# Copying attention's output out of PSUM in one piece, phi's exponentials on VectorE, and zero matmuls in TensorE's idle time

## The chip, the cores and the metric

The kernel runs on one core of one Trainium2 chip. The metric is device time in microseconds (us) of a whole execution; lower is better. The span of a profile is 1.5 to 2 us shorter than the time of the same execution.

## The reference

Two attention blocks read their own inputs of 2048 rows x 1024 columns with 32 heads of 32, and their outputs are laid side by side.

```python
# A: plain attention
qkv = (x @ wqkv).reshape(B, S, 3, H, Dh)
p = softmax(q @ k.T * Dh ** -0.5)
a = (p @ v) @ wo
# B: four segments of 512, causal attention inside a segment, plus a linear memory of the earlier ones
phi = lambda t: where(t > 0, t + 1.0, exp(t))
a_dot = softmax(q_s @ k_s.T * scale + mask) @ v_s
a_mem = (phi(q_s) @ M) / (phi(q_s) @ z + 1e-06)
o = g * a_mem + (1 - g) * a_dot          # g = sigmoid(beta), one per head
M, z = M + phi(k_s).T @ v_s, z + phi(k_s).sum()
b = o @ wo
out = concatenate([a, b])
```

## The kernel before

A small planner runs while the program is built. Generators ask for operations and for buffers (`yield do(...)`, `yield acq(...)`); the planner keeps a clock with an assumed cost for each operation and records one fixed order for each engine. Between the instructions stand waits on semaphores. In the trace of the kernel before, the 23164 records of TensorE and the 1302 of VectorE come in the program's order, compared by their lines of code (one TensorE record is missing): nothing was reordered, and where a wait was not over the engine stood, TensorE for 1.44 us before the scores at 701.76 us.

Four heads are worked on at once. The kernel uses PSUM as eight banks: six, in three pairs, hold scores; the other two (`side`) serve everything else: the accumulation of output and denominator (PV), the projections, the memory of B and the output projection.

```python
PAIRS = [(0, 1), (2, 3), (4, 5)]      # banks of scores
OB, SB = 6, 7                         # Pool "side": all other matmuls
par = dict(b=(14, 10, 3), mem=-4, ..., rate=0.6, ahead=20, sl=5, pv=18, ..., off=0.75, oks=(1, 4, 6), ..., od=8, run=4)
```

A batch of scores fills two pairs; each pair is then emptied by one exponential of 128 x 1024 on ScalarE. For 43 pairs the second half goes to VectorE instead, which computes the exponential with six instructions of bit arithmetic and a polynomial:

```python
def exps(self, u, k, x, pr, sl, one):
    ...
    if (u, k, x) in self.off:                      # 43 of 1184
        Q.spawn(self.exps_dve(pr[1], ...))
        yield do("ACT", ... activation(half, self.ps[:, pr[0], :], ACTF.Exp, scale=sc), ...)
        yield ("ev", other + (0,))                 # the pair is free when VectorE has read it
        Q.give(self.pairs, [pr])
    else:
        yield do("ACT", ... activation(ap, self.ps[:, pr[0]:pr[1] + 1, :], ACTF.Exp, scale=sc), ...)
        Q.give(self.pairs, [pr])
```

When a unit of PV is finished (128 times), one side bank holds the output in its first 256 columns and the denominator in the other 256. Four VectorE operations work on it, and the bank is free only after the last:

```python
def finish(self, u, half, OB, tb):
    den, o = self.ps[:, OB, QU:2 * QU], self.ps[:, OB, 0:QU]
    yield do("DVE", ... transpose(Dt, den) ...)
    yield do("DVE", ... reciprocal(Rc, Dt[:, 0:QU:32]) ...)
    yield do("DVE", ... transpose(Rb, spread(Rc)) ...)
    yield do("DVE", ... tensor_tensor(OTA[...], o, Rb, ALU.mult) ...)
    Q.give(self.side, [OB])                        # only here
```

phi of B takes its exponential on ScalarE (32 instructions), then two VectorE operations:

```python
yield do("ACT", ... activation(self.E[:, k0:k1, :], KQ[:, k0:k1, :], ACTF.Exp) ...)
yield do("DVE", ... tensor_scalar(E, E, 1.0, None, ALU.min) ...)
yield do("DVE", ... scalar_tensor_tensor(PH, KQ, 0.0, E, ALU.max, ALU.add) ...)
```

## Time and profile before

| | before |
|---|---|
| time, median of the first 3 runs | 1156.84 us (1154.09 to 1157.5) |
| span of the profile | 1153.8 us |
| first to last softmax exponential | 16.3 to 1137.9 us |
| mean granted TensorE clock (share of full speed) | 0.985 |

From the page of the kernel before, the busy times by engine and, as the second line, the shares of the chain that ended last:

```profile
PE 1050.9 (91%) x23164; PEld 507.3 (44%) x23165; DVE 626.9 (54%) x1302; ACT 1103.9 (96%) x1223; POOL 127.4 (11%) x285
...
ACT 55%; PE 32%; DVE 7%; DMA 4%; issue 1%; SPq 0%; POOL 0%; DVEq 0%
```

ScalarE (ACT) is busy nearly throughout, but the chain runs through TensorE (PE) for a third of the span: ScalarE's row of exponentials is often released by matmuls.

The groups of ScalarE and VectorE (DVE), shapes kept apart. After the count stand the busy time and the mean length in ns of one, then idle time just before them:

```profile
L891 ACT ACTIVATE PT<-ps 128x1024 bf16<-128x1024 f32 x1125 | 1045.3, 1101 | 21.3 <-PE ps L864 19.2
L885 ACT ACTIVATE PT<-ps 128x512 bf16<-128x512 f32 x43 | 32.0, 744 | 0.0
L718 ACT ACTIVATE E<-KQB 128x1024 bf16<-128x1024 bf16 x16 | 18.1, 1131 | 0.0
L718 ACT ACTIVATE E<-KQB 128x512 bf16<-128x512 bf16 x16 | 11.0, 685 | 0.0
...
L1021 DVE STREAM_TRANSPOSE Rb<-Rall 128x256 f32<-128x256 f32 x128 | 57.0, 445 | 4.2
L1018 DVE STREAM_TRANSPOSE Dt<-ps 128x256 f32<-128x256 f32 x128 | 56.4, 441 | 24.2 <-PE ps L994 23.3
L1025 DVE TENSOR_TENSOR OTA<-ps,Rb 128x256 bf16<-128x256 f32 x64 | 27.1, 423 | 2.1
L1019 DVE RECIPROCAL Rall<-Dt 128x8 f32<-128x8 f32 x128 | 25.8, 202 | 4.0
```

Two readings need care. The mean of one exponential (1101 ns) is not its price: neighbours overlap. In the trace's records the distance from start to start, where nothing was waited for, is 0.904 us for 128 x 1024 and 0.478 us for a half; phi's two forms take 0.947 and 0.520 us. And a group can show no idle time while its engine waits: waits shorter than the overlap (about 0.2 us) vanish in "busy". So throughout this text **work at pace** is the sum of counts times these distances, and **ScalarE's waits** is what the start-to-start distances between the first and the last exponential have beyond that. The whole stretch from the first to the last I call ScalarE's row. Before: 1140 distances x 0.904 + 43 x 0.478 + 16 x 0.947 + 16 x 0.520 = 1075 us of work, 46 us of waits, of which 15 follow the 43 halves.

The four operations that hold the side bank add up to 0.44 + 0.20 + 0.45 + 0.42 = 1.51 us.

Some windows of 20 us: busy time and, in brackets, instructions of PE, PEld, DVE, ACT and POOL, then granted TensorE clock, DMA share, GB/s:

```profile
140.00:160.00 20.00, 18.01 (x404) 8.76 (x396) 11.70 (x25) 18.64 (x22) 1.61 (x4) 0.91 0.36 64
700.00:720.00 20.00, 17.35 (x384) 8.73 (x384) 12.78 (x27) 18.37 (x21) 0.65 (x2) 0.91 0.25 55
740.00:760.00 20.00, 16.08 (x336) 7.32 (x332) 10.27 (x20) 18.69 (x21) 0.00 (x0) 0.91 0.52 94
```

A clock of 0.91 over 20 us is one stretch of 3.4 us at half clock (the trace grants 0.5 for 3.41 us from 148.8 us, from 701.8 us and from 756.4 us). What comes just before such a stretch shows in TensorE's timeline (start, length, engine and line, shape, count, and in brackets the idle time before it and who ended it):

```profile
699.93 0.40 PE L864 MATMUL ps<-QA,KA 32*128 32x256 bf16 x8 [0.38 <-ACT PT L891]
701.76 0.61 PE L864 MATMUL ps<-QA,KA 32*128 32x256 bf16 x8 [1.44 <-ACT PT L891]
702.31 0.41 PE L994 MATMUL ps<-PT,VB 128*32 128x256 bf16 x4
702.49 0.43 PE L994 MATMUL ps<-PT,ones 128*32 128x256 bf16 x4
```

Scores, then 1.44 us of nothing, then scores again: between two batches no other matmul stood in the order; as I read it, because no side bank was free in the plan. Four PV matmuls then take 0.41 us where they take 0.28 us at full clock (as at 42 us in the same trace).

### The profile page before, as it was taken

What the parts mean: (1) busy time and instruction counts of PE and PEld (TensorE: products, weight loads), DVE (VectorE), ACT (ScalarE), POOL (GpSimd) and SP (SyncE); (2) the same over time, 40 slices, a digit from 0 to 9 for tenths busy, and PEclk for the clock granted to TensorE, in tenths of its full rate; (3) what the DMA queues carried; (4) which work ended last, traced back from release to release, by engine and by line L of the source; (5) the groups of instructions that cost most, each with busy time, mean ns of one, the idle gap of its engine ahead of it and who ended that gap; (6) DMA issues with size and microseconds to landing.
All of it is one profiled execution on the core that took longest, in us unless ns stands there. A gap on an engine that the chain in (4) does not pass through costs nothing.

```text
span 1153.8 us, 49786 instructions
## 1 busy us (share of the span) xinstructions
PE 1050.9 (91%) x23164; PEld 507.3 (44%) x23165; DVE 626.9 (54%) x1302; ACT 1103.9 (96%) x1223; POOL 127.4 (11%) x285
## 2 busy tenths in 40 slices
PE   7899998988999988988998998989999899899997
PEld 3444443444444444444444444434444444444454
DVE  1235446545566665755657666556656656635342
ACT  4999999999999999999999999999999999999995
POOL 1001102002011011111111111111111111100000
PEclk9999999999999999999999999999999999989999
DMA  9431342232122122242222232341123111211111
GB/s 178 98 67 36 71 120 49 62 70 62 44 58 48 44 64 46 57 71 48 52 49 57 41 61 48 57 76 44 39 53 63 40 42 30 63 52 39 44 40 51
DMA packets 214841, 67.28 MB, mean 58 GB/s; under 512 B 203872, under 2 KB 212064, under 8 KB 214624
## 3 DMA queue, kind: packets, MB, share of 16 engines
q1 hardware_dynamic: 213296, 63.20, 26.1%
q8 instruction: 184, 3.01, 1.1%
q10 hardware_dynamic: 1328, 0.79, 0.2%
q14 instruction: 33, 0.27, 0.1%
HBM read 36.70 MB, written 8.39 MB: 39 GB/s over the span
## 4 chain that ended last, share of the span: by engine, by line
ACT 55%; PE 32%; DVE 7%; DMA 4%; issue 1%; SPq 0%; POOL 0%; DVEq 0%
ACT PT L891 52%; PE ps L612 12%; PE ps L994 9%; PE ps L864 6%; PE ps L1062 4%; DMA xB<-in_B_x_dram 2%; ACT E L718 1%; DVE Rb L1021 1%; DVE Dt L1018 1%; DMA VA<-VT 1%; DVE ze L916 1%; DVE VT L618 1%; DMA PKt<-PH 1%; ACT PT L885 1%; POOL PT L900 0%
## 5 line engine op out<-in xcount | busy, mean ns | idle before, releaser
L891 ACT ACTIVATE PT<-ps 128x1024 bf16<-128x1024 f32 x1125 | 1045.3, 1101 | 21.3 <-PE ps L864 19.2
L994 PE MATMUL ps<-PT,ones 128*32 128x256 bf16 (+1 forms) x4800 | 296.3, 274 | 0.0
L994 PE MATMUL ps<-PT,VA 128*32 128x256 bf16 x4032 | 252.6, 278 | 17.1 <-ACT PT L891 7.7
L864 PE MATMUL ps<-QA,KA 32*128 32x256 bf16 x4096 | 206.3, 276 | 47.7 <-ACT PT L891 42.6
L612 PE MATMUL ps<-xB,WB 128*32 128x512 bf16 x3072 | 208.1, 387 | 12.0 <-DMA xB<-in_B_x_dram 3.5
L612 PE MATMUL ps<-xA,WA 128*32 128x512 bf16 x3072 | 200.5, 381 | 2.1 <-DVE VT L618 0.5
L900 POOL TENSOR_SCALAR_AFFINE_SELECT PT<-PT 128x256 bf16<-128x256 bf16 (+1 forms) x224 | 99.5, 445 | 835.8 <-ACT PT L891 829.4
L864 PEld LDWEIGHTS ps<-QA,KA 32*128 32x128 bf16 x4096 | 61.0, 92 | 214.6 <-ACT PT L891 192.8
L994 PEld LDWEIGHTS ps<-PT,VA 128*32 128x32 bf16 x4032 | 107.9, 97 | 84.1 <-issue 25.9
L994 PEld LDWEIGHTS ps<-PT,ones 128*32 128x32 bf16 x4800 | 129.9, 98 | 24.5 <-issue 0.3
L612 PEld LDWEIGHTS ps<-xB,WB 128*32 128x32 bf16 x3072 | 72.2, 97 | 92.3 <-issue 45.8
L612 PEld LDWEIGHTS ps<-xA,WA 128*32 128x32 bf16 x3072 | 71.0, 96 | 79.6 <-issue 25.3
L618 DVE CAST VT<-ps 128x512 bf16<-128x512 f32 x64 | 44.1, 688 | 105.9 <-PE ps L612 102.2
L618 DVE CAST KQB<-ps 128x512 bf16<-128x512 f32 x64 | 44.1, 689 | 103.0 <-PE ps L612 103.0
L1068 DVE CAST outsb<-ps 128x512 bf16<-128x512 f32 x61 | 42.1, 690 | 106.6 <-PE ps L1062 106.3
L1018 DVE STREAM_TRANSPOSE Dt<-ps 128x256 f32<-128x256 f32 x128 | 56.4, 441 | 24.2 <-PE ps L994 23.3
L1062 PE MATMUL ps<-WoB,OTB 128*32 128x512 bf16 x1024 | 67.1, 381 | 0.5 <-DVE md L742 0.2
L1062 PE MATMUL ps<-xA,OTA 128*32 128x512 bf16 x1024 | 65.0, 381 | 0.3 <-DVE outsb L1068 0.2
L1021 DVE STREAM_TRANSPOSE Rb<-Rall 128x256 f32<-128x256 f32 x128 | 57.0, 445 | 4.2
L994 PE MATMUL ps<-PT,VB 128*32 128x256 bf16 (+1 forms) x768 | 46.2, 267 | 8.2 <-DVE OTA L1025 3.2
L864 PE MATMUL ps<-KQB 32*128 32x128 bf16 (+3 forms) x512 | 43.4, 302 | 3.9 <-ACT PT L891 2.9
L619 DVE TENSOR_SCALAR QA<-ps 128x512 bf16<-128x512 f32 x32 | 22.0, 688 | 41.0 <-PE ps L612 41.0
(76 smaller groups left out, 658.5 us busy)
## 6 DMA issues: line engine op xcount, KB each, us to landing
WB<-in_B_wk_dram SPq DMA_DIRECT2D x32, 256.0 KB, 3.0
WB<-in_B_wq_dram SPq DMA_DIRECT2D x32, 256.0 KB, 2.9
WB<-in_B_wv_dram SPq DMA_DIRECT2D x32, 256.0 KB, 3.3
out_dram<-outsb SPq DMA_DIRECT2D x64, 128.0 KB, 1.8
WA<-in_A_wqkv_dram SPq DMA_DIRECT2D x23, 256.0 KB, 3.1
WoB<-in_B_wo_dram SPq DMA_DIRECT2D x1, 2048.0 KB, 9.6
xA<-in_A_wo_dram SPq DMA_DIRECT2D x1, 2048.0 KB, 8.4
OTA<-in_A_x_dram ACTq DMA_DIRECT2D x2, 256.0 KB, 4.8
```

The lines of the kernel that those rows point to most:

```text
L612: ins = e.matmul(self.ps[32 * c:32 * c + 32, bank, :], W[:, i, 32 * c:32 * c + 32], x(i), start=(i == 0), stop=(i == NI - 1))
L618: return e.tensor_copy(dst, self.ps[:, bank, :])
L619: return e.tensor_scalar(dst, self.ps[:, bank, :], scale, None, ALU.mult)
L718: yield do("ACT", lambda e: e.activation(self.E[:, k0:k1, :], KQ[:, k0:k1, :], ACTF.Exp), r=kq, w=["E"], cost=0.093 + 0.427 * nk, prio=-1)
L864: ins = e.matmul(self.ps[:, bk, col:col + w], lhs(t, hs), rhs(q0, w, hs), start=True, stop=True)
L891: yield do("ACT", lambda e: e.activation(ap, self.ps[:, pr[0]:pr[1] + 1, :], ACTF.Exp, scale=sc), r=[("ps", bk) for bk in pr], w=keys, cos ...
L900: yield do("POOL", lambda e, m=m, n=n: e.affine_select(m, m, pattern=[[0, n], [1, P]], compare_op=ALU.is_ge, fill=0.0, base=0, channel_mul ...
L994: ins = e.matmul(out, l, r, start=st, stop=sp)
L1018: yield do("DVE", lambda e: e.transpose(Dt[:, :], den), r=[("ps", OB)], w=[("Dt", x)], cost=dve(QU), prio=0, hold=0.15)
L1021: yield do("DVE", lambda e: e.transpose(Rb[:, :].rearrange("p (a b) -> p a b", b=32), self.spread(Rc)), r=[("Rc", ui % 64)], w=[("Rb", x)] ...
L1062: ins = e.matmul(self.ps[32 * c:32 * c + 32, bank, :], lhs(j)[:, 32 * c:32 * c + 32], W(j), start=(j == 0), stop=(j == NG - 1))
L1068: return f(self.outsb[ob][:, :], self.ps[:, bank, :])
```

## The change

The intent: give the side bank back after one copy, so that TensorE always has other work between batches of scores; take phi's exponentials off ScalarE; put the 43 softmax halves back on ScalarE (`off=0`); try to keep TensorE's clock up with matmuls of zero weights in planned idle time; and fit the planner's numbers again.

```diff
-    par = dict(b=(14, 10, 3), mem=-4, ..., rate=0.6, ahead=20, sl=5, pv=18, ..., lead=6, ..., wob=80, off=0.75, oks=(1, 4, 6), sh=4, ..., run=4)
+    par = dict(b=(12, 7, 2), mem=4, ..., rate=0.58, ahead=28, sl=4, pv=24, ..., lead=5, ..., wob=40, off=0, oks=(1, 4), sh=2, ..., run=6, po=(1, 1), fp=2, fil=0.65, fs=0.15)
@@ finish
-        den = self.ps[:, OB, QU:2 * QU]
-        o = self.ps[:, OB, 0:QU]
-        yield do("DVE", lambda e: e.transpose(Dt[:, :], den), r=[("ps", OB)], ...)
+        o = OD[:, 0:QU]
+        yield do("DVE", lambda e: e.tensor_copy(OD[:, :], self.ps[:, OB, :]), r=[("ps", OB)], w=[("OD", x), ("Rb", x)], ...)
+        Q.give(self.side, [OB])
+        yield do("DVE", lambda e: e.transpose(Dt[:, :], Rb), r=[("Rb", x)], ...)
         ... reciprocal, transpose, multiply as before, now from OD in SBUF
-            Q.give(self.side, [OB])
+            Q.give(self.ods, [x])
@@ b_mem (phi)
-        yield do("ACT", lambda e: e.activation(self.E[:, k0:k1, :], KQ[:, k0:k1, :], ACTF.Exp), ...)
+        yield do("DVE", lambda e: e.tensor_scalar(E, KQ[:, k0:k1, :], -84.5, 0.0, ALU.max, ALU.min), ...)
+        for k in range(k0, k1):
+            yield do("DVE", ... tensor_scalar(self.ze, Ek, ONE / math.log(2.0), BIAS, ALU.mult, ALU.add) ...)
+            yield from self.power(Ek, ek, 4)       # the five other steps of exps_dve
@@ planner: when TensorE has nothing ready
+            if eng == "PE" and self.fill:
+                rq = self.fill(soon)               # 4 matmuls of zero weights, if less than 65% of
+                if rq:                             # the last 3.4 us was planned busy; added to an
+                    best = (None, rq)              # open accumulation, so they change nothing
... (cut: more buffers for tB, OD in place of Rb and md, the bookkeeping of open accumulations)
```

## The prediction

> **What bounds the kernel now.** ScalarE's exponentials. The table of busy time has ACT at 1103.9 of 1153.8 us (96%); the chain of waits is 55% ACT. From start to start, an unhindered 128x1024 exponential takes 0.904 us, a 128x512 half 0.478, phi's forms 0.947 and 0.520. The first exponential starts at 16.3 us, the last ends at 1137.9. Between them, work at those paces is 1141 x 0.904 + 43 x 0.478 + 16 x 0.947 + 16 x 0.520 = 1075 us; the other 46 us are ACT waiting: 15 after the 43 halves whose partner goes to VectorE (they come out at 0.836 us, hardly below a full one), 30 after full ones, mostly for the next scores. The tail is 16 us.
>
> **Clock.** Nine stretches inside run at half clock (0.91 to 0.93 in 20-us windows). Each follows 3.4 us in which matmuls filled under 0.38 of TensorE's time (typical: 0.78). [...] In these stretches and the 6 us after them ACT lost 13 us of the 46.
>
> **What the change does** (counted in the two programs' instruction orders).
> - ACT: the 43 softmax halves return to ACT (43 full, no halves), phi's 32 exponentials leave. Work at pace: 1184 x 0.904 = 1070.5 us, only 4 us less. But the 15 us of waits behind halves go.
> - VectorE: minus 43 power chains of 3.57 us (154 us), plus 48 (172 us), plus 128 copies of 128x512 out of PSUM at 0.69 us (88 us): 627 becomes about 735 us, 65%. Not the bound.
> - The output bank is freed after 0.69 us instead of 0.44+0.20+0.45+0.42 = 1.51 us of four operations, 128 times.
> - TensorE: 256 zero matmuls in 64 groups, about 7 us.
> - New order: TensorE work queued between two batches of scores exceeded 1.6 us (estimated from column counts) in 33 places before, now in 3: the start, one early place, and one about three quarters through, where 6.8 us of projections precede a unit of B (K and Q come late, behind the reload of x, which took 8 to 9 us before). There ACT will stand for 5 to 9 us.
>
> **Sum.** Start 16.3 + 1070.5 + tail 17 (the copy adds 0.7 to the last chain) = 1104. Waits: 7 at the late unit, 3 at remaining half-clock stretches, about 10 small ones: 1124, against 1153.8. Nearly all the gain is waiting, not work, and all on the critical path. Most comes from the smoother order that early bank release and the dropped halves allow; fillers give perhaps 5 us, phi's move 4 to 5.
>
> **Prediction: 1125 us**, 8 in 10 between 1110 and 1141. Faster by over 2% 0.76, within 2% 0.22, slower 0.02.
>
> **Right if** ACT has 1184 exponentials at 0.904, no phi, busy about 98%; its waits in sum fall from 46 to 15 to 28 us; mean granted clock rises from 0.985 to at least 0.992, with four stretches or fewer below full; VectorE busy 720 to 750; one visible ACT hole near three quarters.
>
> **Wrong if** VectorE, in order and with chains of 3.6 us, holds back evacuations so that TensorE, also in order, brings scores late; or if the fixed order, fitted to assumed costs, meets late transfers of x and weights and the half clock returns; or the zero matmuls stand before scores that are ready.

## The result, and the profile after

The four runs of the changed kernel had a median of 1140.82 us (1137.05 to 1141.11), those of before 1157.17 us. The ratio is 0.9852, interval 0.9819 to 0.9884: 1.5% less time. Ratios here are the mean time of one kernel's fast runs over that of the other's of the same rounds, so not quite the ratio of the medians quoted. The profiled execution was the fastest of the four: a span of 1135.3 us at a clock of 0.997; the others had 0.993 to 0.994.

The page of the changed kernel, the same two lines:

```profile
PE 1052.0 (93%) x23420; PEld 510.5 (45%) x23421; DVE 719.5 (63%) x1459; ACT 1093.5 (96%) x1192; POOL 140.8 (12%) x286
...
ACT 85%; PE 8%; DVE 3%; SPq 1%; DMA 1%; issue 1%; POOL 0%
```

The chain is now 85% ScalarE: matmuls mostly no longer release the exponentials. The groups, read as before:

```profile
L946 ACT ACTIVATE PT<-ps 128x1024 bf16<-128x1024 f32 x1168 | 1073.1, 1180 | 15.2 <-PE ps L919 15.0
...
L1078 DVE COPY OD<-ps 128x512 f32<-128x512 f32 x128 | 87.1, 681 | 24.4 <-PE ps L1051 23.4
L1084 DVE STREAM_TRANSPOSE OD<-Rall 128x256 f32<-128x256 f32 x128 | 56.6, 442 | 3.4
L1081 DVE STREAM_TRANSPOSE Dt<-OD 128x256 f32<-128x256 f32 x128 | 55.5, 434 | 2.4
L981 DVE SCALAR_TENSOR_TENSOR we<-ue 128x512 f32<-128x512 f32 x48 | 34.3, 715 | 0.0
```

Reading from SBUF makes the transposes no faster (434 against 441 ns); the copy is pure extra work of 87 us on VectorE, and it holds the bank for 0.68 us instead of 1.51. The same windows:

```profile
140.00:160.00 20.00, 19.53 (x460) 9.73 (x456) 12.23 (x28) 20.00 (x23) 1.21 (x3) 1.00 0.31 61
700.00:720.00 20.00, 17.28 (x384) 8.14 (x388) 14.37 (x29) 19.84 (x23) 5.35 (x9) 1.00 0.22 48
740.00:760.00 20.00, 19.23 (x452) 9.55 (x444) 15.40 (x32) 20.00 (x23) 0.00 (x0) 1.00 0.22 48
```

The clock is full and ScalarE has no gap. The larger gaps that are left stand in two places of ScalarE's timeline:

```profile
31.54 24.07 ACT L946 ACTIVATE PT<-ps 128x1024 bf16<-128x1024 f32 x26
57.89 1.94 ACT L946 ACTIVATE PT<-ps 128x1024 bf16<-128x1024 f32 x2 [2.29 <-PE ps L919]
60.93 1.94 ACT L946 ACTIVATE PT<-ps 128x1024 bf16<-128x1024 f32 x2 [1.10 <-PE ps L919]
65.87 20.27 ACT L946 ACTIVATE PT<-ps 128x1024 bf16<-128x1024 f32 x22 [3.00 <-PE ps L919]
...
857.08 10.19 ACT L946 ACTIVATE PT<-ps 128x1024 bf16<-128x1024 f32 x11 [6.40 <-PE ps L919]
```

The second place, 6.4 us before 857, is the late unit of B that the order had shown in advance. The first is explained by TensorE's timeline there:

```profile
53.38 0.29 PE L1051 MATMUL ps<-PT,VA 128*32 128x256 bf16 x3
55.55 0.27 PE L1051 MATMUL ps<-PT,VA 128*32 128x256 bf16 x1 [1.88 <-issue]
...
65.21 0.28 PE L1051 MATMUL ps<-PT,ones 128*32 128x256 bf16 x1 [2.92 <-issue]
```

TensorE stops inside a group of four matmuls that no semaphore divides, "issue" meaning that it waited for nothing the profile shows. This was not foreseen.

ScalarE's account for the profiled execution of every kernel, in us (lead: up to the first exponential; tail: from the start of the last one; parts may miss the span by under 1 us). A profiled execution is not the median one: that of the changed kernel is 3.8 us faster than its kernel's median, that of a_again 1.7 us slower, that of b_off0 1.0 us slower, that of a_old_par_phi_act 2.4 us faster; so differences of 2 or 3 us between two rows say little.

| kernel | lead | work at pace | waits | tail | span |
|---|---|---|---|---|---|
| before | 16.3 | 1074.8 | 46.3 | 17.0 | 1153.8 |
| after | 16.1 | 1069.6 | 33.0 | 16.6 | 1135.3 |
| a_again | 15.8 | 1069.6 | 39.2 | 16.7 | 1140.7 |
| a_ghost_fill | 16.6 | 1069.6 | 33.7 | 16.8 | 1136.7 |
| a_old_finish | 15.9 | 1069.6 | 60.1 | 25.0 | 1170.7 |
| a_phi_act | 15.9 | 1093.1 | 31.4 | 16.7 | 1156.5 |
| a_old_par | 16.1 | 1069.6 | 34.8 | 16.0 | 1135.9 |
| a_old_both | 15.7 | 1069.6 | 54.1 | 15.7 | 1154.7 |
| b_off0 | 15.9 | 1093.1 | 32.8 | 15.9 | 1157.2 |
| a_old_par_phi_act | 16.2 | 1093.1 | 26.3 | 15.7 | 1150.7 |
| a_no_hole | 16.6 | 1069.6 | 27.7 | 15.7 | 1129.1 |
| a_beta | 17.0 | 1069.6 | 30.3 | 17.0 | 1133.2 |
| a_best | 16.4 | 1069.6 | 20.8 | 16.1 | 1122.2 |
| b_fill_fixed | 17.1 | 1074.8 | 43.2 | 16.9 | 1151.9 |

### The profile page after: what moved, and what is told of

Its sections match the earlier page's. It is cut to its first block, busy times and chain, and to the rows that moved or that the text cites. A ratio compares the mean times of both kernels' runs of the same rounds, so it can differ in the third digit from the quotient of the medians.

```text
span 1135.3 us, 50446 instructions
## 1 busy us (share of the span) xinstructions
PE 1052.0 (93%) x23420; PEld 510.5 (45%) x23421; DVE 719.5 (63%) x1459; ACT 1093.5 (96%) x1192; POOL 140.8 (12%) x286
## 4 chain that ended last, share of the span: by engine, by line
ACT 85%; PE 8%; DVE 3%; SPq 1%; DMA 1%; issue 1%; POOL 0%
ACT PT L946 84%; PE ps L655 3%; PE ps L1051 2%; PE ps L1125 2%; PE ps L919 1%; SPq L620 1%; DVE we L981 0%; DMA OTA<-in_A_x_dram 0%; DVE we L982 0%; DMA VA<-VT 0%; DMA PKt<-PH 0%; DVE OD L1078 0%; ACT OTA L946 0%; DVE PH L983 0%; DVE ze L980 0%
## 5 line engine op out<-in xcount | busy, mean ns | idle before, releaser
L946 ACT ACTIVATE PT<-ps 128x1024 bf16<-128x1024 f32 x1168 | 1073.1, 1180 | 15.2 <-PE ps L919 15.0
L919 PE MATMUL ps<-QA,KA 32*128 32x256 bf16 x4096 | 204.0, 273 | 34.0 <-ACT PT L946 26.7
L955 POOL TENSOR_SCALAR_AFFINE_SELECT PT<-PT 128x256 bf16<-128x256 bf16 (+1 forms) x224 | 108.4, 492 | 841.1 <-ACT PT L946 836.2
L655 PE MATMUL ps<-xA,WA 128*32 128x512 bf16 x3072 | 205.6, 382 | 1.8 <-DVE KQB L661 0.9
L655 PE MATMUL ps<-xB,WB 128*32 128x512 bf16 x3072 | 204.0, 382 | 3.2 <-DVE OD L1078 0.9
L1078 DVE COPY OD<-ps 128x512 f32<-128x512 f32 x128 | 87.1, 681 | 24.4 <-PE ps L1051 23.4
L1084 DVE STREAM_TRANSPOSE OD<-Rall 128x256 f32<-128x256 f32 x128 | 56.6, 442 | 3.4
L1081 DVE STREAM_TRANSPOSE Dt<-OD 128x256 f32<-128x256 f32 x128 | 55.5, 434 | 2.4
```

Of the source, the lines that this page charges most:

```text
L655: ins = e.matmul(self.ps[32 * c:32 * c + 32, bank, :], W[:, i, 32 * c:32 * c + 32], x(i), start=(i == 0), stop=(i == NI - 1))
L919: ins = e.matmul(self.ps[:, bk, col:col + w], lhs(t, hs), rhs(q0, w, hs), start=True, stop=True)
L946: yield do("ACT", lambda e: e.activation(ap, self.ps[:, pr[0]:pr[1] + 1, :], ACTF.Exp, scale=sc), r=[("ps", bk) for bk in pr], w=keys, cos ...
L955: yield do("POOL", lambda e, m=m, n=n: e.affine_select(m, m, pattern=[[0, n], [1, P]], compare_op=ALU.is_ge, fill=0.0, base=0, channel_mul ...
L1078: yield do("DVE", lambda e: e.tensor_copy(OD[:, :], self.ps[:, OB, :]), r=[("ps", OB)], w=[("OD", x), ("Rb", x)], cost=dve(2 * QU), prio=0 ...
L1081: yield do("DVE", lambda e: e.transpose(Dt[:, :], Rb), r=[("Rb", x)], w=[("Dt", x)], cost=dve(QU), prio=self.par["fp"], hold=0.15)
```

## The experiments

My theory after the result: the gain is removed waiting, which the early release of the side bank makes possible; phi's move and the fillers add something. The main rival: the fillers keep the clock up (0.985 to 0.994 in the median run), and that is the gain. Names beginning with a_ start from the changed kernel, with b_ from the kernel before. All twelve kernels gave correct results.

### The changed kernel again: a_again

No edit.

> The changed kernel once more, as the yardstick for the three that run beside it. Both theories: 1137 to 1142 us, 0.985 of before, granted clock 0.993 to 0.997, ScalarE's waits between its first and last exponential 33 us or a few more.

Measured: 1140.78 us, ratio 0.9858. It is the yardstick for the next three, which ran beside it.

### The fillers planned but not emitted: a_ghost_fill

TensorE's order without the zero matmuls is the same to the last instruction.

```diff
-        op = self.R.add("SP" if rq.kb else eng, rq.fn, rq.r, rq.w, rq.order, eng)
+        if best[0] is None:
+            op = Op(eng, -1, rq.fn)          # takes its time in the plan, emits nothing
+        else:
+            op = self.R.add("SP" if rq.kb else eng, rq.fn, rq.r, rq.w, rq.order, eng)
```

> The changed kernel with its order kept, but the 64 groups of zero matmuls planned and not emitted. Main theory (gain is the smoother order, which the early bank release allows; fillers are worth about 5 us): 1143 to 1147 us, granted clock 0.988 to 0.992, three to five half-clock stretches more than with fillers. Rival (the clock held up by fillers is the gain): clock back at 0.985 and 1152 to 1157 us. A third outcome, fillers worth nothing: 1139 to 1142, the same clock.

Measured: 1140.57 us, ratio 0.9868, against 1140.78 us beside it; median clock 0.992 against 0.9935. This is the third outcome: in the changed order the fillers are worth nothing that can be measured. My 5 us for them was wrong, and so is the rival: the clock rose because of the order, not because of the fillers.

### The old four operations in PSUM: a_old_finish

The four operations also get back the rank that they had in the planner (`prio=0` instead of `fp`).

```diff
-        yield do("DVE", ... tensor_copy(OD, self.ps[:, OB, :]) ...)
-        Q.give(self.side, [OB])
-        ... transpose, reciprocal, transpose, multiply from OD
+        ... transpose, reciprocal, transpose, multiply from self.ps[:, OB, :], then Q.give(self.side, [OB])
```

> The changed kernel with one part undone: output and denominator are again worked on in PSUM by four VectorE operations, which hold the bank. Main theory: TensorE has fewer banks to work in, so scores come late; 1152 to 1162 us, ScalarE's waits 50 us or more, VectorE busy about 635 us. Rival (fillers, or phi's move, are the gain, the copy is a cost of 88 us of VectorE for nothing): 1136 to 1142 us.

Measured: 1169.83 us, ratio 1.0111: 29 us slower than with the copy, and slower than the kernel before. I had expected 1152 to 1162; the direction is the theory's, the size larger. ScalarE's waits are 60 us, the tail is 8 us longer. Who holds TensorE up shows in its waits in this run (total us, times, longest):

```profile
PE ps L920 <- ACT PT L947: 36.3, 83, 1.4
PE ps L1052 <- DVE tB L1104: 14.6, 22, 1.8
PE ps L1052 <- DVE OTA L1087: 6.1, 8, 1.9
```

and in the changed kernel:

```profile
PE ps L919 <- ACT PT L946: 30.8, 87, 0.8
PE ps L1051 <- ACT PT L946: 9.3, 30, 0.5
PE ps L1051 <- DVE OD L1078: 7.3, 18, 1.1
```

PV waits up to 1.9 us for the multiply that frees the bank; with the copy it waits at most 1.1 us. And while all waits of scores for ScalarE are at most 0.8 us with the copy, they reach 1.4 us without: then, as I read it, TensorE has nothing else it may do, as in the kernel before.

### phi back on ScalarE: a_phi_act

```diff
-    po=(1, 1)
+    po=(0, 1)     # the branch of the changed kernel that keeps the ScalarE exponential
```

> The changed kernel with phi's exponentials back on ScalarE (32 of them, 23.5 us at pace). Main theory: ScalarE is the bound and its waits do not absorb this, so 1157 to 1164 us, as slow as before: phi's move is worth about 20 us, more than the 4 to 5 us of the prediction, which booked it together with the returning halves. Rival (ScalarE's waits absorb half, because the waits come from TensorE's side): 1146 to 1152 us.

Measured: 1156.23 us, ratio 0.9992. The whole gain is gone; the time lies 1 us under the 1157 to 1164 us that the theory gave, and outside the rival's range. The work at pace is 23.5 us more, the waits are 31.4 us instead of 39.2. So with the copy in place phi's move is worth 15.5 us (1156.23 - 1140.78).

### The square of copy and phi

Both parts seem to carry the whole gain, each by itself. To see them apart from the new numbers of the planner I put the old numbers back (`b`, `mem`, `rate`, `ahead`, `sl`, `pv`, `lead`, `wob`, `run`), with no softmax half on VectorE in any corner.

```diff
 a_old_par          = after,  par: numbers of before, off=0
 a_old_both         = a_old_par, and finish() of before
 a_old_par_phi_act  = a_old_par, and po=(0, 1)
 b_off0             = before, par: off=0.75 -> off=0        (both parts old, no fillers)
```

> The changed kernel with the numbers of its planner set back to those of before, except that no softmax half goes to VectorE. The copy out of PSUM, phi on VectorE and the fillers stay. Theory (the early bank release itself lets TensorE be kept in work, whatever the numbers): 1135 to 1146 us. Rival (the new numbers carry the gain): 1150 us or more.

Measured: 1138.65 us, ratio 0.9852. The new numbers carry nothing: with the old ones the ratio is the same as that of the changed kernel (0.9858 in a_again).

> The same old planner numbers, and the old four operations in PSUM as well; phi on VectorE and the fillers stay, no halves. It shows whether the 29 us that the old operations cost under the new numbers are theirs, or come from numbers that were fitted to the copy. Theory (bank release is worth much under either numbers): 1150 to 1160 us, ScalarE's waits 45 us or more. Rival (the 29 us were mostly a misfit of numbers): 1140 to 1147 us.

Measured: 1155.09 us, ratio 0.998, with 54 us of waits. The old operations cost 16 us under the old numbers, 29 under the new ones; the difference goes with the numbers, which had been fitted to the copy. Not all of the 16 us need be the bank's either: this order has a late unit of B of its own, which a_old_par's has not. In ScalarE's timeline:

```profile
861.68 9.27 ACT L947 ACTIVATE PT<-ps 128x1024 bf16<-128x1024 f32 x10 [6.17 <-PE ps L920]
```

> The kernel before with its 43 softmax halves back on ScalarE and nothing else. Work at pace rises by 18.3 us, the 15 us of waits behind halves go. Theory (the halves gained almost nothing): 1150 to 1162 us, ScalarE's waits 25 to 35 us. Rival (the halves were worth their work at pace): 1168 to 1176 us.

Measured: 1157.94 us, ratio 1.0013. The halves had taken 18.3 us of work off ScalarE (43 x (0.904 - 0.478)) and gained nothing clear of noise, as expected: waits fell from 46.3 to 32.8 us when they were undone. The median clock rose to 0.990 against 0.983 beside it, and no time was gained: a higher clock alone is not the gain.

> Completes a square of two by two under the old planner numbers, no softmax half on VectorE in any corner: copy out of PSUM or the old four operations, phi on VectorE or on ScalarE. This is the corner copy, phi on ScalarE. Theory (two limits lie at nearly the same height, ScalarE's work and TensorE's supply of scores; each part of the change lowers one, and only both together gain): 1152 to 1159 us, ScalarE's waits 25 to 33 us. Rival (the copy is worth its 16 us by itself, phi's move little): 1138 to 1144 us.

Measured: 1154.78 us, ratio 0.9992, with 26 us of waits, inside the range of the theory and at the lower end of its waits.

| medians, old numbers, no halves | phi on ScalarE | phi on VectorE |
|---|---|---|
| four operations in PSUM | 1157.94 us | 1155.09 us |
| one copy | 1154.78 us | 1138.65 us |

Either part alone is worth about 3 us, which is not clear of noise (the 95% intervals of the ratios are 0.9994 to 1.0032 for b_off0, 0.9954 to 1.0006 for a_old_both, 0.9969 to 1.0014 for a_old_par_phi_act); both together are worth 19, which is. (The corner at the top left has no fillers, which by a_ghost_fill and b_fill_fixed is at most 4 us, and two buffers for tB where the others have four.) The sizes hold for these orders only: the 6.2 us of the late unit stand in the corner at the top right alone. Without them, as an estimate, phi's move alone would be worth about 9 us and the copy after it about 10; the two together would still give more than their sum of 12. My reading, by ScalarE's account: with four operations in PSUM the row takes 1126 us with phi and 1124 us without (work plus waits), so TensorE's supply sets its length and less work mostly turns into waits (32.8 to 54.1 us, of which 6.2 are the late unit). With phi on ScalarE it takes 1126 us with four operations and 1119 us with the copy (3 of these 7 us come from which executions were profiled), so there the work sets it, and a better supply has little to shorten. Only with both does the row fall to 1104 us. That two limits lie so close is a reading of these accounts; that the two parts together give what neither gives alone is measured.

### Fillers in the kernel before: b_fill_fixed

The fillers were worth nothing measurable in the changed order, whose profiled execution has two stretches at half clock inside. That of the kernel before has nine. Here 103 groups of zero matmuls stand in its planned idle time, at no cost in the plan, so that the rest of TensorE's order is the same to the last instruction.

```diff
+            if eng == "PE" and self.fill:
+                rq = self.fill(soon)
+                if rq:
+                    self.R.add("PE", rq.fn, rq.r, rq.w, None, eng).end = self.now
```

> The kernel before with 103 groups of zero matmuls put where its plan leaves TensorE idle; the rest of TensorE's order is the same to the last instruction. The half-clock stretches lie here, nine of them inside, with 13 us of ScalarE's waits in and behind them. If fillers can hold the clock and that is worth what I counted: granted clock 0.993 or more, 1144 to 1150 us. If they hold the clock but waits stay, because a slow stretch is the mark of a wait and not its cause: clock up, 1153 to 1158 us. If they do nothing: clock 0.985, 1154 to 1158 us.

Measured: 1152.88 us, ratio 0.9963 (0.9944 to 0.9982), median clock 0.987 against 0.984. None of the three outcomes as I put them: the gain is about 4 us and the clock hardly rises. Eight stretches at half clock remain inside; the 3.4 us before them still hold matmul work for 0.39 of the time at most (how this is counted stands in the last section). The fillers stand where the plan is idle, and the chip, as I read it, idles elsewhere too. How much a well aimed filler could give is left open.

### The late unit of B: a_no_hole

The projections of a unit of B wait for the unit two before it, and at the start of a segment that one needs the buffer which the output projection of the previous segment still reads. In the changed kernel's order this comes too late once: the output projection ends at 848 us, the late K and Q projections begin at 850 us, and ScalarE stands for 6.4 us. Other planner numbers avoid it.

```diff
-    rate=0.58, ... sl=4, ... od=8
+    rate=0.59, ... sl=5, ... od=6
```

> The changed kernel with three planner numbers moved a little so that in the plan no unit of B comes late: rate 0.58 to 0.59, od 8 to 6, sl 4 to 5. Theory: the hole of 6.4 us in ScalarE's row near 850 us goes and nothing comes in its place: 1131 to 1136 us. Rival (the hole covers other lateness, which then shows elsewhere): 1138 to 1142 us.

Measured: 1129.46 us (1129.15 to 1130.87), ratio 0.9771: 11 us less than the changed kernel's median (about 9 by the two ratios to the kernel before), better than expected. The hole is gone from ScalarE's timeline, and no new gap of its size came in its place. The other numbers changed the whole order, so not all of the 11 us need be the hole's 6.4.

### TensorE's stops: a_beta

In the trace the 32 values of beta are loaded in 1024 pieces of 2 bytes, from 53.0 to 63.0 us. On the instruction queue a block of 16 KB begins at 52.9 us and the next only at 62.8 us, as the last small pieces end; TensorE stops at 62.3 us. The suspicion: that block holds TensorE's next instructions, and it had to wait for the small pieces. (The trace does not say which engine a block belongs to. The times agree in the other profiled executions: the block begins at 65.1 us and the pieces end at 65.2 in a_again, at 63.0 and 63.1 in a_no_hole.)

```diff
-        for h in range(4):
-            src = AP(beta, offset + h, [[0, 32], [4, 8]])          # 32 x 8 pieces of 2 bytes, four times
-            yield do("SP", dma_start(self.beta[32 * h:32 * h + 32, 0:8], src), ...)
+        src = AP(beta, offset, [[0, 128], [1, 32]])                # 128 rows of 64 bytes, once
+        yield do("SP", dma_start(self.betaw, src), ...)
+        for h in range(4):
+            yield do("DVE", tensor_copy(self.beta[32 * h:32 * h + 32], every fourth of betaw from h), ...)
```

TensorE's order is the same to the last instruction.

> The changed kernel, TensorE's order the same to the last instruction, with the 32 values of beta loaded in one transfer of 128 rows of 64 bytes instead of 1024 pieces of 2 bytes. Theory (TensorE's stops of 1.9 and 2.9 us near 54 and 62 us, which wait for nothing the profile shows, come from its instructions being held up behind those small pieces): the stop near 62 us goes, ScalarE's waits between 45 and 75 us fall from 8 to 3 us, 1134 to 1137 us. Rival (they come from the load of x alone, or belong to the program's length): no change, 1139 to 1142 us.

Measured: 1133.79 us, ratio 0.9798, 7 us less than the changed kernel's median (6 by the two ratios), at the edge of the 1134 to 1137 us expected. ScalarE's waits between 40 and 80 us fell from 7.2 to 2.1 us. From the list of transfers (size, us to landing), the changed kernel and this one:

```profile
beta<-in_B_beta_dram SPq DMA_DIRECT2D x4, 0.5 KB, 7.8
```

```profile
betaw<-in_B_beta_dram SPq DMA_DIRECT2D x1, 8.0 KB, 3.9
```

Each of the four old transfers has a sixteenth of the bytes and takes twice as long. The block of instructions after the one at 53.5 us now begins at 57.1 us, the stop near 62 us is gone, and so is the half-clock stretch of the changed kernel at 56.6 us, which had followed the earlier stop of 1.88 us. ScalarE's timeline has one gap there:

```profile
57.87 23.14 ACT L946 ACTIVATE PT<-ps 128x1024 bf16<-128x1024 f32 x25 [1.31 <-PE ps L919]
```

Of that earlier stop 1.40 us stay near 55 us; it lies at the end of the load of x and is left open. The kernel before has the same small pieces, and the next block begins at 63.1 us there too, but TensorE waited 2.1 us for the load of x in that time and stopped for only 0.95 us at 65.

### Both repairs: a_best

The edits of a_no_hole and a_beta together.

> Both repairs together: the planner numbers without the late unit of B, and beta in one transfer. Theory: 1122 to 1126 us, 0.972 of before, ScalarE's waits about 21 us. Rival (the stops move on with the schedule): 1128 to 1131 us.

Measured: 1123.97 us (1122.82 to 1126.71), ratio 0.9719: 2.8% faster than the kernel before, and the best of all. Waits of ScalarE that the view of waits still shows:

```profile
ACT PT L946 <- PE ps L919: 2.6, 6, 1.3
```

and for the changed kernel:

```profile
ACT PT L946 <- PE ps L919: 15.0, 10, 6.4
```

## Why the prediction was right or wrong

The time, 1140.82 us, lies inside the range, but by 0.2 us: two of the four runs were above 1141, so that it lies inside is luck. The central 1125 us and the 76% for "over 2% faster" were too hopeful. The gain was half of what I had summed. (The sum was also one of a span, which is about 1.7 us shorter than the time that it was given for.)

- **The bound: right. The kind of gain: right as an account, not as a cause.** Against the kernel before, the work at pace fell by 5 us (the prediction said 4), the waits by 13 us in the profiled execution; of the 16 us between the medians that leaves 11 for waits. The chain went from 55% to 85% ScalarE. But b_off0, as slow as the kernel before, has 32.8 us of waits, as many as the changed kernel's 33.0: seen from there the gain is phi's 23.5 us of work, whose removal the copy keeps from turning into waits. The waits did not fall to the 15 to 28 us named, and ScalarE was busy 96%, not 98%.
- **The order as evidence: right.** "33 places before, now 3" was read from the two orders before any run, and the late unit came out at 6.4 us, inside the 5 to 9 us stated. The clock rose to 0.994 in the median run as forecast. The profiled execution had two half-clock stretches inside the span; that of a_again had four.
- **VectorE: just below the range.** 719.5 us against "720 to 750": the chain of six instructions took 3.44 us for phi instead of the 3.57 us for scores.
- **The mis-sized term: "about 10 small ones".** The sum had waits of 7 for the late unit, 3 for half clock and 10 for the rest, 20 in all. The profiled execution had 33.0: 6.8 in the 20 us of the late unit, 7.3 between 40 and 80 us, 1.3 at another half-clock stretch, 17.6 for the rest, so the last term was short by 7.6. The 7.3 us between 40 and 80 us are TensorE's stops and the half-clock stretch behind them, which no term held; a_beta took away 5 of them in its profiled execution, and 7 us of the median time. The profiled execution was also the fastest of four: that of a_again, the slowest of its six, had 39.2 us of waits.
- **Fillers "perhaps 5 us": wrong.** Emitting them or not makes no measurable difference (a_ghost_fill).
- **"phi's move 4 to 5": wrong as a share.** I booked it as work, net of the returning halves. Alone it is worth 3 us (within noise, and about 9 but for a late unit), together with the copy 15.5 to 16. The same holds for the copy: 3 us alone, 16 to 29 with phi's move, late units and misfit of the planner's numbers included. Where the parts work only together, a sum of shares is the wrong form.
- **"The smoother order that early bank release and the dropped halves allow": half right.** The early release matters, together with phi's move. The halves gave and cost nothing (b_off0), and the new numbers of the planner added nothing (a_old_par).

## What to carry to other kernels

When an engine is 96% busy and the chain still runs through another engine for a third of the span, two limits may lie at nearly the same height, as here: test the parts of a change in a square, since each alone may look worthless. A PSUM bank that feeds long VectorE work can be worth emptying with one plain copy, even at the price of more VectorE work (87 us here), if VectorE has room (it was 54% busy before and 63% after) and TensorE has too few banks (two here for all but the scores); here it paid 16 us with phi's move and 3 without. Before taking a difference between two fixed orders for the effect of an edit, look for a late unit that only one of them has. Compare the fixed orders before a run for long stretches of other work between the instructions that feed the bounding engine, and look at every transfer of tiny pieces, however few its bytes (here 2 KB in 1024 pieces; with one transfer in their place the median was 7 us lower).

## What else the runs show of the clock, zero matmuls and small transfers

- In the 3.4 us ahead of the nine half-clock stretches of the kernel before, TensorE's longest gap was 0.5 to 2.1 us. I count work by taking a group of four matmuls of 256 columns as 0.107 us, the planner's cost (at full clock the trace has such groups 0.11 us apart), and other shapes in proportion. The 3.4 us ahead of these stretches then held work for 0.16 to 0.38 of the time (0.19 to 0.39 in b_fill_fixed), where a typical 3.4 us hold 0.78. The starts of the stretches lie whole multiples of 3.41 us apart in the traces of the kernel before and of the changed one. Of the windows of 3.41 us on that grid, away from the start and the end, every one under 0.34 was followed by half clock in these two traces, and some of 0.34 to 0.42 were not. Off the grid it does not hold: in the changed kernel the 3.4 us up to 65.2 us, with TensorE's stop of 2.92 us in them, held under 0.1, and full clock followed. So no sharp limit is shown, and the forecast's "under 0.38" is what stood ahead of the nine, not a limit. Eight of the nine stretches last 3.41 us, one 6.83.
- Planned zero matmuls were worth nothing in one order (1140.57 against 1140.78 us) and about 4 us in another (ratio 0.9963), where eight half-clock stretches stayed.
- A stop of TensorE went with the small pieces. While 1024 pieces of 2 bytes were under way on the DMA engines (53.0 to 63.0 us), a block of 16 KB on the instruction queue began only at 62.8 us, as the last piece ended (57.1 us without the pieces), TensorE stopped for 2.9 us, and the time fell by 7 us when the pieces went. That the block held TensorE's instructions is not shown.
- Pieces of 2 bytes were slow: 0.5 KB of them took 7.8 us to land, 8 KB in rows of 64 bytes 3.9 us. With them the next block of instructions, on another queue, began 5.7 us later.
